# A tiled recurrence with a feed-forward layer: three leading blocks loaded, turned and ordered in another way

## The chip, the core and the metric

The kernel runs on one core of a Trainium2 chip. A core has a tensor engine (PE, which multiplies matrices and turns tiles), a vector engine (DVE), a scalar engine (ACT, for exponentials, logarithms and SiLU), a general engine (POOL) and SP, whose queue starts most transfers. Each engine works through its own list of instructions in order; semaphores hold an instruction back until what it needs is there. [...] The metric is the device time of one run in microseconds (us). Lower is better.

## What is computed

The first half is a gated recurrence over 768 tokens for 4 batches and 8 heads of 48 channels, the second a feed-forward layer on its output (3072 tokens of 384 channels, 2048 hidden).

```python
f = 1.0 / (1.0 + np.exp(-f_logit))
for t in range(S):
    state = f[:, :, t, :, None] * state + np.einsum('bhd,bhe->bhde', k[:, :, t], v[:, :, t])
    y[:, :, t] = np.einsum('bhd,bhde->bhe', q[:, :, t], state)
...
h = x @ w_in
g = h * (1.0 / (1.0 + np.exp(-h)))
return (g @ w_out).astype(np.float32)
```

Inputs and output are fp32.

## The kernel before

**Units.** A unit is 128 tokens of one batch with all its heads; there are 24, worked on in pairs. For each unit the recurrence is done with matrix products. `E` and `L` make the log of the gates on ACT (an exponential, then a logarithm); `cs` (or `csh`) sums them over the tokens on PE with a triangular matrix; `a`, `ia` and `al` are exponentials of the sums; `qg` and `ki` multiply q and k by them; `tq` turns both on PE into PSUM, and `qc`, `kc` or `qkc` copy the result to SBUF (units from 8 on use a transposing DMA, `qkD`, instead); `sc2` makes the scores of a pair, `at` masks them on the way out of PSUM, and `y` sums scores times v and the turned q times the state of the batch's last unit. `d`, `sd` and `su` bring that state on.

**Feed-forward.** `yc`, `yT` and `xc` (or `yD`, again a transposing DMA) turn y; `mi1` (units 0 to 5, one unit at a time, 12 matmuls of 128 columns, a quarter of the hidden layer) or `mi` (a pair, 6 matmuls of 256 columns, an eighth) make the hidden layer, `si1` and `si` apply SiLU on ACT, and `mo` adds a quarter of the output (4 matmuls of 384 columns). `oc` and `so` copy and store it. The weights come in fp32 through `wi` and `wo` into staging tiles and are cast by `wic` and `woc`.

**The first three pairs** (units 0 to 5) are loaded as blocks of 256 successive tokens of one batch: partition p of a tile gets tokens 2p and 2p+1, so that a piece of memory is 384 bytes. Each of the two slots of such a tile holds the tokens of one parity, of both units. v was loaded in the plain way, token by partition, and the turned k was put back into token order by a copy with a stride of two (`kc`), while q was left sorted by parity (`qc`).

**The order** of all engines is written out by hand, as a long table of words (`PLAN`): a word is the step, its unit, its engine and the buffers that it takes. The program emits the steps in that order, engine by engine; ACT gets a table load where exponentials and SiLU follow one another. Idle matmuls on zeros (`idle`) fill places in the head.

Steps in the code: loads L257, weights L295 and L299, `E` L264, `L` L266 (blocks) and L268, `idle` L291, `csh` L335 to L339, `cs` L372 and L376, `ia` L379, `a` L381, `tq` L395, the transposing DMAs L407 and L442, `dT` L411, `at` L416, `y` L422 and L426, `yT` L434, `d` L448, `sd` L453 and L455, `mi1` L313, `si1` L310, `mi` L323, `si` L320, `mo` L351, the last halves of `mo` L357, stores L364 and L369. Copies, casts and products stand at the lines of helpers: L235 (ACT), L237 (DVE), L239 (POOL), L242 (products).

Of the kernel before, what the change touches and what calls it, by code (L numbers as in the profile page):

```python
# [36 lines left out]
kn_0/ACT/0 d_0/PE/2 wi_1/SP/0 wi_0/SP/1 at_0_1/DVE/0 at_0_0/DVE sd_0/DVE/0 at_1_0/DVE/1 su_0/POOL/0 idle_4_2_256/PE/1 y_0/PE/3 tq_3/PE/1,5
idle_5_2_256/PE/2 tq_2/PE/2,0 wo_0/SP/1 a_4/ACT/1 ia_5/ACT/1 al_4/ACT/2 kc_3/ACT/1 at_1_1/DVE qc_3/DVE vb_1/ACT/1 a_5/ACT/2 yc_0/ACT/0 ia_4/ACT/2
kc_2/DVE qc_2/DVE y_1/PE/7 dT_2/PE/5 yT_0/PE/1 sc2_1/PE/6,0,3,2 wo_1/SP/2 wic_2_2/POOL wic_2_0/POOL yc_1/DVE/1 wic_2_1/ACT vb_2/ACT/2 xc_0/DVE/0
at_2_0/DVE/2 at_2_1/DVE dT_1/PE/4 yT_1/PE/7 dT_3/PE/1 mi1_0_1/PE/6 wi_4/SP/3 y_2/PE/0 xc_1/ACT wic_1_0/ACT wic_0_0/ACT kn_1/DVE/1 kn_2/DVE/0  # L40
yc_2/DVE/2 at_3_0/DVE/3 wic_1_1/POOL wic_0_1/POOL mi1_1_1/PE/7 d_2/PE/4 yT_2/PE/5 mi1_0_0/PE/0 mi1_1_0/PE/3 wi_3/SP/4 si1_0_1/ACT/0 si1_1_0/ACT
si1_0_0/ACT sd_2/DVE/1 xc_2/DVE/1 woc_0_2/DVE woc_0_1/DVE woc_0_0/DVE v_3/SP woc_1_2/DVE mi1_2_1/PE/4 mi1_2_0/PE/5 mo_1_0/PE/6 mo_0_0/PE/3 d_1/PE/0
si1_2_1/ACT/1 si1_2_0/ACT kn_3/ACT/0 woc_1_0/POOL si1_1_1/ACT wic_4_0/POOL wic_4_1/POOL wic_4_2/ACT at_3_1/DVE woc_1_1/DVE su_2/DVE/0 wic_3_1/DVE
sd_1/DVE/0 wic_3_2/POOL mo_2_0/PE/4 q_4_5/SP/2 k_4_5/SP/2 mo_1_1/PE mo_0_1/PE mo_2_1/PE mi1_0_3/PE/5 mi1_2_3/PE/1 mi1_1_3/PE/2 wo_2/SP/0 wic_3_0/ACT
vb_3/POOL/3 mi1_1_2/PE/7 y_3/PE/0 si1_0_3/ACT si1_2_3/ACT si1_1_2/ACT yc_3/DVE/0 qg_4/POOL/4 wo_3/SP/1 mi1_2_2/PE/5 d_3/PE/1 ki_4/POOL sd_3/DVE/1
yT_3/PE/7 mi1_0_2/PE/0 si1_2_2/ACT si1_0_2/ACT xc_3/DVE tq_4/PE/5,1 mi1_3_3/PE/7 mi1_3_2/PE/0 kc_4/ACT/2 si1_1_3/ACT qc_4/DVE si1_3_3/ACT si1_3_2/ACT
qg_5/DVE/0 ki_5/POOL tq_5/PE/5,1 mi1_3_0/PE/2 mi1_3_1/PE/7 f_6/SP/3 v_4/SP/2 f_8_9/SP/0 v_5/SP f_7/SP qc_5/ACT si1_3_0/ACT si1_3_1/ACT woc_2_2/POOL
woc_2_0/DVE woc_2_1/DVE kc_5/DVE mo_2_2/PE sc2_2/PE/0,5,2,1 dT_4/PE/7 mo_0_2/PE at_5_1/DVE/0 su_3/DVE/0 su_1/DVE/0 kn_4/DVE/1 at_5_0/DVE at_4_0/DVE/1
at_4_1/DVE woc_3_1/ACT woc_3_0/POOL woc_3_2/POOL vb_4/POOL/4 E_6/ACT L_6/ACT/0 E_8_9/ACT q_6/SP/3 v_6/SP/3 k_6/SP/3 mo_2_3/PE mo_1_2/PE mo_3_0/PE/1
mo_0_3/PE cs_6/PE/7 mo_3_1/PE d_4/PE/2 y_4/PE/0 a_6/ACT/0 L_8_9/ACT/1 yc_4/ACT/1 E_7/ACT ia_6/ACT/0 vb_5/DVE/5 oc_0/DVE/0 sd_4/DVE/1 su_4/DVE/0  # L50
mo_3_2/PE cs_9/PE/5 cs_8/PE/3 yT_4/PE/2 mo_1_3/PE y_5/PE/0 L_7/ACT al_9/ACT/3 al_6/ACT/4 a_8/ACT/1 ia_9/ACT/2 al_8/ACT/5 ia_8/ACT/1 a_9/ACT/2
oc_1/ACT/1 xc_4/DVE/2 yc_5/DVE/2 f_10_11/SP/1 q_7/SP k_7/SP q_8_9/SP/0 k_8_9/SP/0 f_12_13/SP/2 v_7/SP cs_7/PE/2 dT_5/PE/7 mo_3_3/PE yT_5/PE/0
kn_5/DVE/0 xc_5/DVE qg_6/POOL/1 ki_6/POOL vb_6/POOL/0 ia_7/ACT/0 a_7/ACT/0 al_7/ACT/6 E_10_11/ACT L_10_11/ACT/2 mi1_4_0/PE/3 mi1_4_1/PE/7 d_5/PE/5
tq_6/PE/6 qkc_6/DVE/0 oc_3/DVE/2 sd_5/DVE/0 oc_2/DVE/3 qg_7/DVE/3 ki_7/DVE mi1_4_2/PE/0 mi1_5_2/PE/2 mi1_5_1/PE/6 d_6/PE/1 mi1_4_3/PE/5 mi1_5_0/PE/4
si1_4_2/ACT/2 si1_5_1/ACT si1_4_0/ACT si1_5_0/ACT mi1_5_3/PE/0 tq_7/PE/6 mo_4_0/PE/3 mo_5_0/PE/4 sd_6/DVE/1 qkc_7/DVE qg_9/POOL/2 su_6/POOL/0
so_2/POOL v_8_9/SP/0 si1_5_3/ACT si1_4_1/ACT si1_5_2/ACT si1_4_3/ACT sc2_3/PE/1,0,6,7 q_12_13/SP/1 ki_8/POOL/4 at_6_1/DVE/2 ki_9/DVE at_6_0/DVE
at_7_1/DVE/3 at_7_0/DVE so_3/POOL vb_7/POOL/2 mo_5_1/PE cs_11/PE/2 mo_4_1/PE cs_10/PE/5 mo_4_2/PE y_6/PE/0 mo_4_3/PE d_7/PE/1 y_7/PE/7 E_12_13/ACT
al_11/ACT/7 a_10/ACT/0 L_12_13/ACT/1 al_10/ACT/0 yc_6/DVE/0 yc_7/ACT/1 oc_4/DVE/4 qg_8/POOL sd_7/DVE/1 cs_12/PE/6 cs_13/PE/0 yT_6/PE/3 mo_5_2/PE
yT_7/PE/1 ia_11/ACT/0 a_12/ACT/2 ia_12/ACT/1 ia_13/ACT/2 al_13/ACT/1 a_13/ACT/1 al_12/ACT/4 vb_9/POOL/1 xc_6/DVE/3 xc_7/DVE mo_5_3/PE mi_3_3/PE/7
d_9/PE/3 qkD_9/SP/1 qkD_8/SP f_14_15/SP/0 qg_12/DVE/0 su_7/POOL/0 vb_8/POOL/3 oc_5/DVE/3 sd_9/DVE/1 q_10_11/SP/2 k_10_11/SP/1 a_11/ACT/2 mi_3_0/PE/1  # L60
mi_3_4/PE/0 mi_3_5/PE/6 mi_3_6/PE/4 mi_3_1/PE/2 si_3_3/ACT/0 si_3_4/ACT si_3_5/ACT si_3_0/ACT si_3_1/ACT si_3_6/ACT su_5/POOL/0 qg_11/POOL/1
sc2_4/PE/3,7,0,6 mi_3_2/PE/1 mi_3_7/PE/2 at_9_0/DVE/1 at_8_1/DVE/0 at_8_0/DVE at_9_1/DVE si_3_2/ACT si_3_7/ACT mo_7_0/PE/4 mo_7_1/PE y_8/PE/0 y_9/PE/7
mo_7_2/PE mo_7_3/PE mo_6_0/PE/1 yc_8/DVE/2 ki_11/DVE qg_10/DVE/3 E_14_15/ACT yc_9/ACT/0 L_14_15/ACT/0 ia_10/ACT/0 ki_10/POOL k_12_13/SP/2 v_10_11/SP/1
qkD_11/SP/2 qkD_10/SP yT_9/PE/3 yT_8/PE/2 mo_6_1/PE cs_15/PE/6 mo_6_2/PE a_15/ACT/2 ia_15/ACT/0 al_15/ACT/6 xc_9/DVE/0 xc_8/DVE mi_4_1/PE/0
mi_4_0/PE/7 mi_4_2/PE/5 mi_4_3/PE/3 mi_4_6/PE/2 d_8/PE/6 mo_6_3/PE si_4_2/ACT/1 vb_10/ACT/4 si_4_1/ACT si_4_0/ACT si_4_3/ACT si_4_6/ACT sd_8/DVE/0
ki_12/DVE vb_11/DVE/5 v_14_15/SP/2 f_16_17/SP/3 k_14_15/SP/3 q_14_15/SP/3 mi_4_5/PE/5 mi_4_4/PE/0 sc2_5/PE/6,7,3,2 oc_6/DVE/2 qg_13/POOL/2 so_0/POOL
ki_13/POOL so_1/POOL su_9/POOL/0 qg_15/POOL/4 si_4_4/ACT si_4_5/ACT at_10_1/DVE/2 at_10_0/DVE at_11_0/DVE/3 su_8/POOL/0 at_11_1/DVE mo_8_0/PE/1
mi_4_7/PE/0 si_4_7/ACT cs_14/PE/5 mo_8_1/PE y_10/PE/7 mo_8_2/PE y_11/PE/6 d_11/PE/3 mo_9_0/PE/0 yc_10/DVE/1 yc_11/DVE/0 al_14/ACT/2 oc_7/ACT/0
E_16_17/ACT L_16_17/ACT/2 yT_10/PE/2 mo_8_3/PE yT_11/PE/7 mo_9_1/PE cs_16/PE/4 xc_10/ACT/1 oc_8/ACT/1 ia_14/ACT/2 a_16/ACT/0 al_16/ACT/3 a_14/ACT/1
ia_16/ACT/1 qg_14/POOL/1 xc_11/DVE sd_11/DVE/1 mi_5_3/PE/6 d_10/PE/2 mi_5_6/PE/7 mo_9_2/PE mi_5_4/PE/1 mi_5_1/PE/3 mi_5_0/PE/5 si_5_6/ACT/2 si_5_3/ACT  # L70
si_5_4/ACT si_5_0/ACT si_5_1/ACT qkD_13/SP/0 qkD_12/SP v_12_13/SP/3 q_16_17/SP/0 ki_14/DVE sd_10/DVE/0 su_10/DVE/0 ki_15/DVE qkD_15/SP/1 so_5/SP
qkD_14/SP f_18_19/SP/1 mi_5_2/PE/4 sc2_6/PE/2,7,6,1 mi_5_5/PE/5 mo_9_3/PE mi_5_7/PE/3 vb_13/POOL/0 at_12_1/DVE/0 at_13_1/DVE/1 vb_12/ACT/2 si_5_2/ACT
vb_14/DVE/1 su_11/POOL/0 at_13_0/DVE at_12_0/DVE si_5_7/ACT si_5_5/ACT d_12/PE/7 cs_17/PE/4 mo_11_0/PE/1 mo_11_1/PE mo_11_2/PE y_12/PE/6 d_13/PE/3
mo_10_0/PE/2 y_13/PE/5 mo_10_1/PE sd_12/DVE/0 yc_12/DVE/2 oc_9/DVE/3 sd_13/DVE/1 yc_13/DVE/1 a_17/ACT/2 al_17/ACT/5 ia_17/ACT/2 vb_15/ACT/3 yT_12/PE/7
mo_10_2/PE yT_13/PE/4 sc2_7/PE/6,0,3,5 E_18_19/ACT xc_12/DVE/2 su_13/DVE/0 L_18_19/ACT/1 xc_13/DVE f_20_21/SP/2 so_7/SP v_16_17/SP/0 v_18_19/SP/1
k_16_17/SP/0 at_14_1/DVE/2 at_15_0/DVE/3 at_15_1/DVE at_14_0/DVE mo_10_3/PE mi_6_1/PE/7 mi_6_7/PE/4 mi_6_6/PE/0 mo_11_3/PE y_14/PE/3 y_15/PE/5
# [454 lines left out]
```

## Time and profile before

| | |
|---|---|
| median of 3 runs | 178.46 us (177.73 to 179.22) |
| the profiled execution | 177.89 us |
| its span, first to last instruction | 176.1 us |
| read from memory, written | 25.17 MB, 4.72 MB |
| mean rate | 200 GB/s |
| DMA packets | 115541, of them 110752 under 512 bytes |
| ACT table loads | 18, 1.28 us each |

A profile's row in order of time has start, duration, engine, line, operation, output <- input, shapes and count, and in brackets how long the engine was idle before and what ended that. In rows of groups, the first number behind the bar is the busy time, the second the mean duration in ns of one. The chain of waits is followed back from the last instruction: at each step to what released it. Neighbouring matmuls overlap, so the pace of a row of matmuls is told by the time from start to start.

### The profile page before, as it was taken

What the parts mean: (1) busy time and instruction counts of PE and PEld (TensorE: products, weight loads), DVE (VectorE), ACT (ScalarE), POOL (GpSimd) and SP (SyncE); (2) the same over time, 40 slices, a digit from 0 to 9 for tenths busy, and PEclk for the clock granted to TensorE, in tenths of its full rate; (3) what the DMA queues carried; (4) which work ended last, traced back from release to release, by engine and by line L of the source; (5) the groups of instructions that cost most, each with busy time, mean ns of one, the idle gap of its engine ahead of it and who ended that gap; (6) DMA issues with size and microseconds to landing.
All of it is one profiled execution on the core that took longest, in us unless ns stands there. A gap on an engine that the chain in (4) does not pass through costs nothing.

```text
span 176.1 us, 4798 instructions
## 1 busy us (share of the span) xinstructions
PE 169.5 (96%) x1952; PEld 133.6 (76%) x1952; DVE 97.7 (55%) x201; ACT 133.3 (76%) x249; POOL 59.1 (34%) x91
## 2 busy tenths in 40 slices
PE   7998799999999999999999999999999999999992
...
PEclk9999999999999999999999999999999999999999
DMA  5999998998999999999899994999675975950222
GB/s 147 325 286 259 397 387 220 397 207 169 217 199 241 182 238 221 159 233 232 152 197 165 251 227 89 273 176 210 137 153 99 206 162 138 217 147 0 92 90 89
DMA packets 115541, 35.17 MB, mean 200 GB/s; under 512 B 110752, under 2 KB 113056, under 8 KB 115520
## 3 DMA queue, kind: packets, MB, share of 16 engines
...
q8 instruction: 15, 0.25, 0.5%
...
HBM read 25.17 MB, written 4.72 MB: 170 GB/s over the span
## 4 chain that ended last, share of the span: by engine, by line
PE 73%; SPq 8%; DMA 8%; DVE 5%; issue 2%; POOL 2%; ACT 0%; POOLq 0%; DVEq 0%
PE ps L351 27%; PE ps L323 22%; PE ps L313 8%; SPq L257 6%; DMA wh<-in_moe_w_in_dram 5%; PE ps L280 3%; PE ps L357 3%; DMA qkT<-qk 3%; PE ps L426 2%; SPq L442 2%; DVE st L242 2%; PE ps L422 2%; PE ps L372 1%; DVE at L416 1%; PE ps L448 1%
## 5 line engine op out<-in xcount | busy, mean ns | idle before, releaser
L351 PE MATMUL ps<-w_out,hT 128*128 128x384 bf16 x352 | 66.4, 326 | 0.0
L323 PE MATMUL ps<-xT,w_in 128*128 128x256 bf16 x432 | 52.4, 273 | 0.0
L323 PEld LDWEIGHTS <-w_in 128*128 128x128 bf16 x432 | 45.3, 110 | 3.9 <-DMA xT<-yb 0.3
L320 ACT ACTIVATE hT<-ps 128x512 bf16<-128x512 f32 x72 | 39.0, 603 | 10.3 <-PE ps L323 9.6
L351 PEld LDWEIGHTS <-hT 128*128 128x128 bf16 x352 | 31.7, 97 | 16.6 <-ACT hT L310 0.3
L416 DVE TENSOR_TENSOR at<-ps,triu 128x512 bf16<-128x512 f32 x36 | 22.5, 683 | 19.8 <-PE ps L280 18.8
L242 POOL TENSOR_TENSOR qk<-q,av 128x384 bf16<-128x384 f32 x15 | 15.4, 1033 | 42.2 <-DMA q<-in_q_dram 25.0
L499 ACT ACT_TABLE_LOAD x17 | 21.8, 1283 | 0.3
L313 PE MATMUL ps<-xT,w_in 128*128 128x128 bf16 x288 | 17.9, 219 | 0.9 <-POOL w_in L239 0.6
L313 PEld LDWEIGHTS <-w_in 128*128 128x128 bf16 x288 | 16.6, 110 | 1.3 <-POOL w_in L239 0.8
L242 POOL TENSOR_TENSOR qk<-k,ia 128x384 bf16<-128x384 f32 x12 | 12.7, 1066 | 13.4 <-DMA k<-in_k_dram 8.7
L381 ACT ACTIVATE av<-ps 128x384 f32<-128x384 f32 x24 | 11.9, 504 | 3.5 <-PE ps L376 1.8
L237 DVE CAST yb<-ps 128x384 bf16<-128x384 f32 x16 | 8.8, 555 | 10.2 <-PE ps L426 9.0
L264 ACT ACTIVATE f<-f 128x768 f32<-128x768 f32 (+1 forms) x13 | 10.3, 796 | 5.4 <-DMA f<-in_f_logit_dram 5.3
L310 ACT ACTIVATE hT<-ps 128x512 bf16<-128x512 f32 x24 | 13.2, 607 | 1.6 <-PE ps L313 1.5
L453 DVE TENSOR_TENSOR sd<-ps,st 128x384 f32<-128x384 f32 x16 | 8.8, 553 | 9.5 <-ACT hT L320 4.7
L369 POOL DMA_DIRECT2D out_dram<-ob x14 | 8.0, 573 | 17.9 <-DVE ob L237 14.3
L242 POOL TENSOR_TENSOR st<-sd,al 48x192 bf16<-48x192 f32 x18 | 9.8, 543 | 8.7 <-PE ps L422 5.1
L379 ACT ACTIVATE ia<-ps 128x384 f32<-128x384 f32 x24 | 11.8, 505 | 0.0
L237 DVE COPY ob<-ps 128x384 f32<-128x384 f32 x14 | 7.7, 553 | 7.4 <-PE ps L351 3.6
L239 POOL CAST vb<-v 128x384 bf16<-128x384 f32 x11 | 5.6, 507 | 14.6 <-DMA v<-in_v_dram 13.2
L242 DVE TENSOR_TENSOR qk<-k,ia 128x384 bf16<-128x384 f32 x12 | 7.1, 605 | 5.1 <-ACT ia L379 4.2
...
## 6 DMA issues: line engine op xcount, KB each, us to landing
...
```

The costliest lines, as they stand in the source:

```text
L237: nc.vector.tensor_copy(o, i)
L242: (nc.vector if eng == "DVE" else nc.gpsimd).tensor_mul(*a)
L257: nc.sync.dma_start(out=dst, in_=src)
L310: return nc.scalar.activation(at("hT", u // 2)[:, 4 * m:4 * m + 4, i * C:(i + 1) * C], h, AF.Silu)
L313: nc.tensor.matmul(h[:, n, :], w_in_tile(4 * m + n, kk), at("xT", u // 2)[:, kk, i * C:(i + 1) * C], start=(kk == 0), stop=(kk == KT - 1))
L320: return nc.scalar.activation(at("hT", P)[:, 2 * j:2 * j + 2, :], h, AF.Silu)
L323: nc.tensor.matmul(h[:, i, :], w_in_tile(2 * j + i, kk), at("xT", P)[:, kk, :], start=(kk == 0), stop=(kk == KT - 1))
L351: nc.tensor.matmul(o, at("hT", P)[:, n, i * C:(i + 1) * C], w_out_sb[n // 4][:, n % 4, :], start=(n == 0), stop=(n == NT - 1))
L379: nc.scalar.activation(at("ia", u).rearrange("p h d -> p (h d)"), at("cs", u)[:, 0:HD], AF.Exp)
L381: nc.scalar.activation(at("av", u).rearrange("p h d -> p (h d)"), at("cs", u)[:, 0:HD], AF.Exp, scale=-1.0)
L416: nc.vector.tensor_mul(at("at", u)[:, r], at(f"s{r}", u).rearrange("p (n c) -> p n c", c=C), (triup if two else triu)[:, None, :].to_broad ...
L499: nc.scalar.preload_act_table_set(turn[n])
```

## The change

- `v` of units 0 to 5 is loaded sorted by parity, in two DMAs of 64 partitions each; the turned q and k then both stay sorted, and one copy (`qkc`) takes both out of one PSUM bank. The mask `triup` is built to match.
- `E` and `L` of the three blocks work on half of the heads at a time (`Eh`, `Lh`), and a load may take half of the heads: `f_0_1` is loaded so, heads 4 to 7 first.
- The set `BLOCKS` replaces the number `HALF` (the same three pairs), and `APART` goes. Weights may be loaded straight by POOL, and scores one unit at a time; the new table uses neither.
- `PLAN` is new throughout: engines, buffers and order.

```diff
-HALF = 3
-
-APART = {0, 1, 2, 3, 4, 5}
+BLOCKS = {0, 1, 2}
...
-f_0_1/SP/0 f_2_3/SP/1 k_0_1/SP/0 q_0_1/SP/0 E_0_1/ACT L_0_1/ACT/0 E_2_3/ACT idle_0_11_512/PE/0 csh_0/PE/0,1 f_4_5/SP/2 q_2_3/SP/1 v_0/SP/0 k_2_3/SP/1
...
+f_0_1_1/SP/0 f_0_1_0/SP f_2_3/SP/1 q_2_3/SP/0 q_0_1/SP/1 k_0_1/SP/0 Eh_0_0/ACT Eh_0_1/ACT Lh_0_1/ACT/0 Lh_0_0/ACT idle_0_12_512/PE/0 csh_0/PE/0,1
...
-        if u // 2 < HALF and n == 2:
...
+        if u // 2 in BLOCKS and n >= 2:
+            hs = slice(0, H) if n == 2 else slice(4 * us[2], 4 * us[2] + 4)
+            dst = at(x, u // 2).rearrange("p a h d -> p (a h d)").rearrange("p (h w) -> p h w", h=H)[:, hs]
+            src = SRC[x][b, hs, c * C:(c + 2) * C, :].rearrange("h (p s) d -> p h (s d)", s=2)
+        elif u // 2 in BLOCKS:
+            for s in range(2):
+                nc.sync.dma_start(out=at(x, u // 2)[64 * s:64 * (s + 1), u % 2],
+                                  in_=SRC[x][b, :, c * C:(c + 1) * C, :].rearrange("h (p s) d -> s p h d", s=2)[s])
+            return
...
+    def half_logs(kind, u, hf):
+        P, hs = u // 2, slice(4 * hf, 4 * hf + 4)
+        if kind == "Eh":
+            e = at("f", P).rearrange("p a h d -> p (a h d)").rearrange("p (h w) -> p h w", h=H)[:, hs]
+            nc.scalar.activation(e, e, AF.Exp, scale=-1.0)
+        else:
+            nc.scalar.activation(at("lf", P)[:, :, hs, 0:D], pairs("f", P)[:, :, hs], AF.Ln, bias=1.0)
...
         elif kind == "qkc":
-            copy(eng, at("qkT", P)[:, 1024 * i:1024 * (i + 1)], bank16("tq", u))
-        elif kind in ("qc", "kc"):
...
-            copy(eng, dst, bank16("tqk" if j and u in APART else "tq", u)[:, 512 * j:512 * (j + 1)].rearrange("p (w c) -> p w c", c=64))
+            if two:
+                copy(eng, at("qkT", P).rearrange("p (w s c) -> p s w c", s=2, c=64)[:, i],
+                     bank16("tq", u).rearrange("p (w c) -> p w c", c=64))
+            else:
+                copy(eng, at("qkT", P)[:, 1024 * i:1024 * (i + 1)], bank16("tq", u))
...
-        nc.vector.tensor_copy(triup.rearrange("p (s c) -> p s c", s=2), triu.rearrange("p (c s) -> p s c", s=2))
...
+        for s in range(2):
+            r = slice(64 * s, 64 * (s + 1))
+            nc.vector.tensor_copy(triup[r, 64:128], tri2[r, r])
+            nc.vector.tensor_copy(triup[r, 0:64], (tri2s if s else tri2)[r, r])
```

What the table moves is seen best in the lists of the engines. On SP's queue, from the last loads of the first two pairs on to the weights, the program of before has (tiles f_71, q_78 and k_74 are those of pair 2 or 1; ws and wh stage weights):

```order
L257 DMA f_71<-in_f_logit_dram 128x8x96
L257 DMA q_78<-in_q_dram 128x8x96
L257 DMA v_81<-in_v_dram 128x8x48
L257 DMA k_74<-in_k_dram 128x8x96
L257 DMA v_82<-in_v_dram 128x8x48
L257 DMA v_81<-in_v_dram 128x8x48
L295 DMA ws_85<-in_moe_w_in_dram 128x3x512
L295 DMA wh_90<-in_moe_w_in_dram 128x3x256
```

And the changed one:

```order
L262 DMA k_73<-in_k_dram 128x8x96
L262 DMA k_74<-in_k_dram 128x8x96
L256 DMA v_81<-in_v_dram 64x8x48 x2
L262 DMA f_71<-in_f_logit_dram 128x8x96
L256 DMA v_81<-in_v_dram 64x8x48 x2
L256 DMA v_82<-in_v_dram 64x8x48 x2
L316 DMA ws_85<-in_moe_w_in_dram 128x3x512
L316 DMA ws_86<-in_moe_w_in_dram 128x3x512
```

The third block's f moves behind the k of the first two, each v comes as two halves, and two large weight loads follow one another where a large one and two small ones did.

On ACT, at the start (f_69 is the gate tile of pair 0, f_70 of pair 1), before:

```order
L264 ACTIVATE f_69<-f_69 128x768
L266 ACTIVATE lf_92<-f_69 128x16x48
L264 ACTIVATE f_70<-f_70 128x768
L266 ACTIVATE lf_93<-f_70 128x16x48
L379 ACTIVATE ia_95<-ps_61 128x384
```

And now:

```order
L279 ACTIVATE f_69<-f_69 128x384 x2
L281 ACTIVATE lf_92<-f_69 128x2x4x48 x2
L279 ACTIVATE f_70<-f_70 128x384 x2
L281 ACTIVATE lf_93<-f_70 128x2x4x48 x2
L404 ACTIVATE av_98<-ps_61 128x384
```

Each step has become two, and `a` comes ahead of `ia`.

On DVE, between the first states and the first output weights (sd_122 and sd_123 are sums for a state, w_in_160 to 162 and w_out_163 the cast weights, yb and xT the y of units), before:

```order
L237 CAST yb_121<-ps_61 128x384
L416 TENSOR_TENSOR at_118<-ps_64,triup 128x512
L455 COPY sd_123<-ps_65 128x384
L237 COPY xT_140<-ps_66 128x3x2x64
L237 CAST w_out_163<-ws_86 128x512 x3
L237 CAST w_out_164<-ws_87 128x512
```

And now:

```order
L236 CAST w_in_162<-ws_86 128x512 x2
L241 TENSOR_TENSOR st_147<-sd_123,al_124 48x4x48 x2
L435 TENSOR_TENSOR at_118<-ps_63,triup 128x512
L236 CAST w_in_160<-ws_87 128x512 x2
L236 CAST w_in_159<-wh_90 128x384
L236 CAST w_in_158<-wh_91 128x384
L236 CAST w_out_163<-ws_88 128x512 x3
L236 CAST vb_109<-v_82 128x384
L236 CAST w_out_164<-ws_89 128x512
```

All of the hidden layer's weights are cast before the output's, DVE casts six pieces of them where it cast one, and the v of unit 3 (vb_109) is cast between the first and the second output weight.

More of the change, by code (lines that the diff above doesn't have):

```diff
@@ L37 @@
[L37 to L76, printed above, removed]
@@ L101 @@
-moh_23_0_0/PE/2 moh_23_0_1/PE moh_23_0_2/PE moh_23_0_3/PE moh_22_0_2/PE moh_22_0_3/PE moh_22_1_1/PE moh_22_1_2/PE moh_22_1_3/PE moh_23_1_1/PE
-och_22_0/ACT/3 och_23_0/ACT/1 oc_18/DVE/4 och_22_1/ACT moh_23_1_2/PE moh_23_1_3/PE so_18/SP so_21/POOL so_20/POOL soh_23_0/SP soh_22_1/SP soh_22_0/SP
-och_23_1/ACT soh_23_1/SP
+f_0_1_1/SP/0 f_0_1_0/SP f_2_3/SP/1 q_2_3/SP/0 q_0_1/SP/1 k_0_1/SP/0 Eh_0_0/ACT Eh_0_1/ACT Lh_0_1/ACT/0 Lh_0_0/ACT idle_0_12_512/PE/0 csh_0/PE/0,1
+Eh_2_1/ACT Eh_2_0/ACT Lh_2_1/ACT/1 Lh_2_0/ACT k_2_3/SP/1 v_0/SP/0 f_4_5/SP/2 v_1/SP v_2/SP/1 idle_1_5_256/PE/2 csh_1/PE/2,3 a_0/ACT/0 a_1/ACT/1
@@ new lines @@
+at_1_0/DVE kn_1/DVE/0 wi_2/SP/2 at_2_0/DVE/2 at_2_1/DVE dT_3/PE/1 d_1/PE/6 yT_0/PE/7 d_2/PE/4 y_1/PE/0 xc_0/ACT/0 Lh_4_0/ACT kn_3/DVE/0 wi_1/SP/0
+wi_0/SP/1 wic_3_2/POOL wic_3_0/POOL y_2/PE/3 yc_1/ACT/1 yc_2/DVE/2 wic_3_1/ACT csh_2/PE/7,1 yT_2/PE/0 yT_1/PE/3 xc_2/ACT/1 sd_2/DVE/1 at_3_1/DVE/3
+sd_1/DVE/0 xc_1/ACT mi1_0_2/PE/4 mi1_2_2/PE/5 mi1_1_2/PE/0 wic_4_0/ACT wo_0/SP/3 wic_4_2/DVE wic_4_1/DVE su_2/DVE/0 at_3_0/DVE wo_1/SP/4 mi1_1_3/PE/3
+mi1_2_3/PE/6 mi1_0_3/PE/2 wic_2_2/POOL si1_1_2/ACT/0 si1_0_2/ACT wic_2_1/DVE wic_2_0/DVE si1_1_3/ACT si1_0_3/ACT si1_2_3/ACT/1 wic_1_1/DVE
```

128 lines of the change are left out of this document (85 added, 43 removed).

## The prediction

> **What bounds the kernel now.** I read the page first: busy time of the engines and the 40 slices.
>
> ```profile
> span 176.1 us, 4798 instructions
> ...
> PE 169.5 (96%) x1952; PEld 133.6 (76%) x1952; DVE 97.7 (55%) x201; ACT 133.3 (76%) x249; POOL 59.1 (34%) x91
> ...
> PE   7998799999999999999999999999999999999992
> ...
> PEclk9999999999999999999999999999999999999999
> DMA  5999998998999999999899994999675975950222
> ```
>
> The tensor engine (PE) is busy everywhere but in the first five slices (22 us) and the last; its clock is full in all of them. The change takes no matrix work away: the order of both programs has the same matmuls, save the idle ones on zeros (26 before, 31 now). So its end moves only by time in which it does nothing useful. I read the chain of waits next, for where that time ends.
>
> ```profile
> 12.72 8.02 DMA wh<-in_moe_w_in_dram
> ...
> 20.77 0.52 ACT w_in L235
> ...
> 21.34 2.85 PE ps L313 x48
> ...
> 25.66 2.65 PE ps L351 x16
> 28.31 2.68 PE ps L313 x48
> ...
> 173.02 0.32 ACT ob L235
> ```
>
> Up to 21.34 the chain runs through the queue of SP and a weight transfer; from there nearly all of it is PE work, to 173.0. The rows also price a step: 2.65 / 4 = 0.66 us for one `mo` (4 matmuls) and 2.68 / 4 = 0.67 us for one `mi1` (12 matmuls). PE's timeline shows the head.
>
> ```profile
> 5.98 0.32 PE L335 MATMUL ps<-lf,tri 128*128 128x384 bf16 x1 [0.22 <-ACT lf L266]
> ...
> 11.89 0.62 PE L280 MATMUL ps<-qkT 48*128 48x128 bf16 x16
> ...
> 17.03 0.62 PE L280 MATMUL ps<-qkT 48*128 48x128 bf16 x16
> ...
> 18.96 0.86 PE L313 MATMUL ps<-xT,w_in 128*128 128x128 bf16 x12 [0.59 <-POOL w_in L239]
> 19.66 0.36 PE L426 MATMUL ps<-vb,at 128*128 128x48 bf16 x8
> ...
> 20.54 0.33 PE L448 MATMUL ps<-vb,kn 128*128 128x96 bf16 x4
> 20.71 0.33 PE L434 MATMUL ps<-ident,yb 128*128 128x128 bf16 x3
> ```
>
> First scores at 11.89, second at 17.03, first hidden layer (`mi1`) at 18.96, waiting for weights. What sets that is when the weights land: the instructions that cast each piece stand idle until its DMA.
>
> ```profile
> 17.64 0.62 ACT L235 CAST w_in<-ws 128x512 bf16<-128x512 f32 x1 [0.78 <-DMA ws<-in_moe_w_in_dram]
> ...
> 22.73 1.10 DVE L237 CAST w_out<-ws 128x512 bf16<-128x512 f32 x3 [0.55 <-DMA ws<-in_moe_w_out_dram]
> ...
> 24.67 0.87 POOL L239 CAST w_out<-ws 128x512 bf16<-128x512 f32 x1 [3.36 <-DMA ws<-in_moe_w_out_dram]
> 26.70 1.18 POOL L239 CAST w_in<-ws 128x512 bf16<-128x512 f32 x2 [1.15 <-DMA ws<-in_moe_w_in_dram]
> 29.25 0.87 POOL L239 CAST w_in<-ws 128x512 bf16<-128x512 f32 x1 [1.38 <-DMA ws<-in_moe_w_in_dram]
> ```
>
> Six weight loads of 768 KB (the two 384 KB ones count as one, at 20.77 in the chain) land at 17.6, 20.8, 22.7, 24.7, 26.7 and 29.2 us. Each gives PE three units' work, 3 x 0.67 = 2.0 us, so loads and work run at almost the same pace.
>
> **The change, part by part.**
>
> *Does the first weight land earlier?* It is behind the same pieces on SP. Its queue:
>
> ```profile
> 7.79 1.15 SPq L257 DMA_DIRECT2D k<-in_k_dram  x1
> 8.99 2.03 SPq L257 DMA_DIRECT2D v<-in_v_dram  x2
> 11.06 1.08 SPq L295 DMA_DIRECT2D ws<-in_moe_w_in_dram  x1
> 12.18 1.03 SPq L295 DMA_DIRECT2D wh<-in_moe_w_in_dram  x2
> ```
>
> A `k` of 384 KB holds it 1.15 us, a `v` of 192 KB 2.03 / 2 = 1.02, a `wh` of 384 KB 0.52. The first two have 1024 pieces each (128 partitions x 8 heads), `wh` 384. Cost follows pieces, not bytes. Halving a load (`f_0_1`, and three `v` ahead of the weights) keeps the pieces, so I take nothing; from above, halves at the `wh` price of 0.52 would add 3 x (2 x 0.52 - 1.02) = 0.06 us, and the worst case is a rival below. Below nothing, no piece goes away. The first weight still lands at 17.6.
>
> *Exponentials and logarithms by halves.* One whole pair on ACT:
>
> ```profile
> 4.21 0.84 ACT L264 ACTIVATE f<-f 128x768 f32<-128x768 f32 x1 [2.19 <-DMA f<-in_f_logit_dram]
> 5.08 0.84 ACT L266 ACTIVATE lf<-f 128x768 bf16<-128x768 f32 x1
> 5.83 0.83 ACT L264 ACTIVATE f<-f 128x768 f32<-128x768 f32 x1
> ...
> 7.44 0.85 ACT L379 ACTIVATE ia<-ps 128x384 f32<-128x384 f32 x2
> ```
>
> Two of 384 columns take 0.85 us, one of 768 takes 0.84: halving costs 0.01 us each time. The gain would be an earlier start, but the second half of the heads is loaded first while ACT starts with the first half, so it still waits for both, until 4.2. The chain of four then ends near 6.0 as before (5.92): term 0, between -0.4 (half a load less to wait for) and +0.2. [...]
>
> *Turned q and k in one copy.*
>
> ```profile
> L237 DVE COPY qkT<-ps 128x512 bf16<-128x512 bf16 x8 | 4.2, 570 | 0.3 <-PE ps L395 0.2
> ...
> L237 DVE COPY qkT<-ps 128x1024 bf16<-128x1024 bf16 x2 | 1.4, 692 | 1.8 <-PE ps L395 1.8
> ```
>
> Two copies of 0.57 become one of 0.69: 0.45 us less for each unit that DVE copies, and one PSUM bank less. Larger is what the order does with it. The k of units 2 and 3 came late:
>
> ```profile
> 12.76 1.95 POOL L242 TENSOR_TENSOR qk<-k,ia 128x384 bf16<-128x384 f32 x2
> ```
>
> It was done at 14.7, and the second scores came 2.3 us behind. Now `k_2_3` is loaded two places sooner (2 x 1.15 us) and DVE makes both; then the last of the four is unit 3's q on POOL (1.0 us), near 13.0, and 2.3 us more put the second scores at about 15.3. So `d_1`, `d_2`, `y_2` and `yT_2` are done when the first weight is there. By the starts above a `d` or `yT` is 0.17 us (20.54 to 20.71) and a `y` without a state 20.54 - 0.67 - 19.66 = 0.21, so 0.72 for the four. Before, `d_1` came later still, and the other three (0.55) lay with two `mi1` (1.34) between 18.96 and 21.34: 2.38 - 1.34 - 0.55 = 0.49 us of waiting for the next weights. With three `mi1` at hand on the first load, that wait isn't met at once. So the head can win 0.72 + 0.49 = 1.2 us: the same 18.96 with more behind it, and no hole right after.
>
> *What is late next.* The new order lets all 12 `mi1` of units 0 to 2 run ahead of the `mo`, on the six landings. PE would be through the first load's work at 18.96 + 2.01 = 20.97. The second is there at 20.8 and its two casts on DVE take some 0.8 (three took 1.10): PE starts at 21.6, waiting 0.65. Third: 22.7 + 0.85, PE free at 23.6: no wait. Fourth, 24.7 + 0.9: 25.6 against 25.6. Fifth: 26.7 + 1.1 = 27.8 against 27.6, 0.2. Then three `mo` to 29.8, and `y_3` needs `v_3`, which lands last:
>
> ```profile
> 16.28 2.33 SPq L257 DMA_DIRECT2D v<-in_v_dram  x1
> ...
> DMA to landing us min/median/max: 13.5/13.5/13.5
> ```
>
> 16.28 + 13.5 = 29.8; its cast, 0.4: PE waits some 0.4 us, since `y_3` stands ahead of two `mo` that could run (the old order put it behind them). Sum of what is given back: 0.65 + 0.2 + 0.4 = 1.25; bounds 0.4 (the second load lands 0.8 sooner, as nothing small is in it) to 2.0.
>
> *The old order's own holes.* After 28 us PE has a few of its own.
>
> ```profile
> 32.89 0.91 PE L395 MATMUL ps<-ident,qk 128*128 128x128 bf16 x8
> ...
> 34.97 0.61 PE L395 MATMUL ps<-ident,qk 128*128 128x128 bf16 x8
> ```
>
> The turning of unit 4 takes 0.30 us more than that of unit 5: its k is late from POOL. In the new order DVE makes that k, with time to spare. I take 0.3 won, between 0 and 0.6, since the steps around it move too.
>
> *The middle and the end.* One hole is a transposing DMA:
>
> ```profile
> PEld L280 <- DMA qkT<-qk: 0.3, 1, 0.3
> ...
> L407 SPq DMA_TRANSPOSE qkT<-qk x16: 1231/1269/3565, 57.0 to 148.7; - x16
> ```
>
> Everything else is moved, with two ACT table loads more (1.28 each), under which PE has other work. The last scores come closer behind their transposes: by the plan's listing some 3.9 us of PE work lies between the two, 7.8 before. I take 0 for the middle, between -0.3 and +2.5. The end (half `mo`, copy, store) is the same.
>
> **Sum** against the profiled execution, 177.89 us (span 176.1 and 1.8 around it): -1.2 + 1.25 - 0.3 = -0.25, so 177.6. That is 0.5% under the median of the runs shown, 178.46. They spread from 177.7 to 179.2, so about 1% is what a measurement of this kernel can tell from no change.
>
> **Rivals.**
>
> *The weights keep up* (faster): none of the 1.25 us comes back. For it: the second landing of before was two loads of 384 KB, and a single one may be quicker. 177.89 - 1.2 - 0.3 = 176.4, 1.2% under the median.
>
> *Halves of v cost as much as whole ones* (slower): each of the three extra `v` DMAs ahead of the weights holds the queue 1.15 us. For it: 64 partitions and 192-byte pieces are a form the trace does not show, and `k` and `v` cost about the same at twice the bytes. Against it: `wh`, at 0.52. The weights land 3 x 1.15 = 3.5 us late, PE waits all of it: 177.6 + 3.5 = 181.1. It counts from 0.9 us more for each `v` (3 x 0.9 = 2.6 above the forecast). [...]
>
> *Transposes late in the middle* (slower): pair 5's scores now follow pair 4's after 6 us of PE work instead of 13, and the last are close, too. If three of these places wait 1 us each, 177.6 + 3 = 180.6; it needs 0.9 us at each to count. Against it: one load instead of five now stands on SP between pair 4's transposes and pair 5's.
>
> *The head does nothing* (the halves are late anyway, the two copies were hidden, weights rule): 177.9, no change.
>
> **How the numbers follow.** Forecast 177.6: 0.34. Head does nothing, 177.9: 0.20. Weights keep up, 176.4: 0.24. Transposes late, 180.6: 0.12. Halves of v, 181.1: 0.10. Faster by over 1% (under 176.7): 0.24. Slower by over 1% (over 180.2): 0.22. Within: 0.54. The range takes in the gains at their bounds (177.89 - 1.2 - 0.6 - 0.3 in the middle = 175.8) and reaches up to the first of the slower rivals, where about half of their chance lies: 175.8 to 180.6.
>
> **What would show it.** Right, if the first `mi1` starts within 0.5 us of 18.96 with four more steps behind it, the second scores start near 15.3, and PE has holes before the second load's `mi1` and before `y_3`. The halves of `v` are told by when SP comes to the first weight load, 11.06 before. Wrong, if that passes 12, if the first scores pass 12.4, or if PE shows waits of over 0.7 us ahead of scores after 50 us. If the first `mi1` of unit 4 starts over 1 us sooner than before, the give-back was overrated.

## The result, and the profile after

| | before | after |
|---|---|---|
| median of 20 runs each | 178.16 us (177.16 to 179.22) | 179.53 us (178.46 to 181.48) |
| ratio, 95% interval | 1 | 1.0074 (1.0048 to 1.0100) |
| the profiled execution, its span | 177.89, 176.1 us | 178.59, 176.8 us |

The changed kernel is 0.7% slower, some 1.3 us. The forecast was 177.6, a small gain. The page of the changed kernel shows PE as full as before:

```profile
span 176.8 us, 4813 instructions
...
PE 170.2 (96%) x1957; PEld 134.4 (76%) x1957; DVE 103.3 (58%) x210; ACT 138.2 (78%) x257; POOL 47.4 (27%) x74
```

SP's queue in order of time (start, time that the issue held the queue) shows where the difference begins. Before, up to the first v:

```profile
0.74 1.08 SPq L257 DMA_DIRECT2D f<-in_f_logit_dram  x2
1.87 1.11 SPq L257 DMA_DIRECT2D k<-in_k_dram  x1
3.02 1.15 SPq L257 DMA_DIRECT2D q<-in_q_dram  x1
4.21 1.15 SPq L257 DMA_DIRECT2D f<-in_f_logit_dram  x1
5.41 1.15 SPq L257 DMA_DIRECT2D q<-in_q_dram  x1
6.60 1.15 SPq L257 DMA_DIRECT2D v<-in_v_dram  x1
```

And now, up to the weights:

```profile
0.74 1.55 SPq L262 DMA_DIRECT2D f<-in_f_logit_dram  x3
2.33 3.05 SPq L262 DMA_DIRECT2D q<-in_q_dram  x2
5.43 2.34 SPq L262 DMA_DIRECT2D k<-in_k_dram  x2
7.81 1.85 SPq L256 DMA_DIRECT2D v<-in_v_dram  x2
9.71 0.62 SPq L262 DMA_DIRECT2D f<-in_f_logit_dram  x1
10.38 3.12 SPq L256 DMA_DIRECT2D v<-in_v_dram  x4
13.54 1.68 SPq L316 DMA_DIRECT2D ws<-in_moe_w_in_dram  x3
```

The same bytes go out, but SP comes to the first weight at 13.54 instead of 11.06, 2.48 us late. Half of that is there at the first v (7.81 instead of 6.60): the two q hold SP for 3.05, where two loads of that size took 2.30 before. The other half comes from there to the first weight (5.73 us instead of 4.46), with the three v in halves. Here the hold of one load isn't its price: the halves hold 4.97 where whole ones took 1.15 + 2.03, but the f between them holds only 0.62 where the k of before took 1.15. So places several loads further on are compared below. PE's own timeline, and the chain of waits up to the end of the head:

```profile
13.40 0.62 PE L293 MATMUL ps<-qkT 48*128 48x128 bf16 x16 [0.70 <-DVE qkT L236]
...
17.18 0.62 PE L293 MATMUL ps<-qkT 48*128 48x128 bf16 x16
...
21.01 8.20 PE L334 MATMUL ps<-xT,w_in 128*128 128x128 bf16 x144
...
32.21 0.36 PE L445 MATMUL ps<-vb,at 128*128 128x48 bf16 x8 [0.44 <-DVE vb L236]
```

```profile
2.96 2.43 SPq L262
...
20.15 0.61 SPq L256
...
20.80 10.90 DMA v<-in_v_dram
...
31.80 0.37 DVE vb L236
...
32.21 0.36 PE ps L445 x8
32.56 0.77 PE ps L374 x4
```

Followed back from the end, the chain is PE work to 32.21, then unit 3's v, its transfer of 10.90 us, and from there SP's issues one after the other to the start; the longest is the second q, 2.43. Before, it left the loads at 21.34, with a weight. So in the new order the last load that the head needs, not a weight, releases PE. Ahead of its first `mi1` at 21.01 PE shows no wait; it comes there late from the scores, which start at 13.40 instead of 11.89.

### The profile page after: what moved, and what is told of

It reads as the page before. It is cut to its first block, busy times and chain, and to the rows that moved or that the text cites. A ratio compares the mean times of both kernels' runs of the same rounds, so it can differ in the third digit from the quotient of the medians.

```text
span 176.8 us, 4813 instructions
## 1 busy us (share of the span) xinstructions
PE 170.2 (96%) x1957; PEld 134.4 (76%) x1957; DVE 103.3 (58%) x210; ACT 138.2 (78%) x257; POOL 47.4 (27%) x74
## 3 DMA queue, kind: packets, MB, share of 16 engines
q0 software_dynamic: 576, 1.77, 2.9%
## 4 chain that ended last, share of the span: by engine, by line
PE 80%; SPq 11%; DMA 6%; issue 1%; DVE 0%; ACT 0%; DVEq 0%
PE ps L374 32%; PE ps L344 27%; DMA v<-in_v_dram 6%; PE ps L334 5%; SPq L262 4%; PE ps L293 3%; SPq L256 3%; PE ps L380 3%; PE ps L445 2%; SPq L316 2%; PE ps L441 2%; PE ps L395 2%; PE ps L467 2%; SPq L320 1%; PE ps L453 1%; PE ps L418 1%
## 5 line engine op out<-in xcount | busy, mean ns | idle before, releaser
L374 PE MATMUL ps<-w_out,hT 128*128 128x384 bf16 x352 | 65.0, 326 | 0.0
L341 ACT ACTIVATE hT<-ps 128x512 bf16<-128x512 f32 x72 | 38.5, 603 | 11.5 <-PE ps L344 11.2
L241 POOL TENSOR_TENSOR qk<-q,av 128x384 bf16<-128x384 f32 x12 | 13.2, 1110 | 36.8 <-ACT av L404 25.1
L236 DVE COPY ob<-ps 128x384 f32<-128x384 f32 (+1 forms) x15 | 7.7, 527 | 14.2 <-PE ps L374 8.3
L241 DVE TENSOR_TENSOR st<-sd,al 48x192 bf16<-48x192 f32 x24 | 13.9, 577 | 0.8 <-PE ps L441 0.6
L241 POOL TENSOR_TENSOR st<-sd,al 48x192 bf16<-48x192 f32 x16 | 8.9, 554 | 18.9 <-DVE sd L472 11.6
L331 ACT ACTIVATE hT<-ps 128x512 bf16<-128x512 f32 x24 | 12.8, 602 | 0.9 <-PE ps L334 0.7
L241 DVE TENSOR_TENSOR qk<-q,av 128x384 bf16<-128x384 f32 x12 | 9.1, 762 | 6.6 <-ACT av L404 6.5
L241 POOL TENSOR_TENSOR qk<-k,ia 128x384 bf16<-128x384 f32 x8 | 8.3, 1043 | 15.2 <-DMA k<-in_k_dram 10.4
L236 DVE CAST yb<-ps 128x384 bf16<-128x384 f32 x13 | 6.9, 552 | 7.7 <-PE ps L445 5.9
L241 DVE TENSOR_TENSOR qk<-k,ia 128x384 bf16<-128x384 f32 x16 | 9.5, 610 | 2.8 <-DMA k<-in_k_dram 2.1
```

The lines of the kernel that those rows point to most:

```text
L236: nc.vector.tensor_copy(o, i)
L241: (nc.vector if eng == "DVE" else nc.gpsimd).tensor_mul(*a)
L331: return nc.scalar.activation(at("hT", u // 2)[:, 4 * m:4 * m + 4, i * C:(i + 1) * C], h, AF.Silu)
L341: return nc.scalar.activation(at("hT", P)[:, 2 * j:2 * j + 2, :], h, AF.Silu)
L374: nc.tensor.matmul(o, at("hT", P)[:, n, i * C:(i + 1) * C], w_out_sb[n // 4][:, n % 4, :], start=(n == 0), stop=(n == NT - 1))
```

## The experiments

The ratios are to the kernel before, with 95% intervals. "SP" is the time at which SP comes to the first weight load, "`mi1`" the start of the first hidden layer, from one profiled execution each. That execution can lie away from the median (by 1.6 us for f in halves: 178.22 against 179.80), so the sizes are read from the ratios and the places from the profile. In the three runs of the changed order with v in one piece and the copy as it was (third, fifth and fourteenth row) v no longer matches the sorted scores, so their output is not the right one; the work is the same.

| run | ratio | SP | `mi1` |
|---|---|---|---|
| before | 1 | 11.06 | 18.96 |
| after | 1.0074 (1.0048 to 1.0100) | 13.54 | 21.01 |
| after, v in one piece | 0.9973 (0.9938 to 1.0008) | 11.99 | 21.27 |
| after, f in one piece | 1.0000 (0.9963 to 1.0037) | 12.22 | 20.12 |
| after, both in one piece | 0.9950 (0.9918 to 0.9982) | 11.36 | 20.08 |
| after, `E` and `L` whole | 1.0071 (1.0037 to 1.0106) | 13.93 | 21.74 |
| before, v in halves of partitions | 1.0061 (1.0025 to 1.0097) | 12.85 | 20.38 |
| before, v in halves of heads | 1.0027 (0.9992 to 1.0062) | 11.86 | 19.34 |
| before, f in halves of heads | 1.0066 (1.0032 to 1.0100) | 11.59 | 19.54 |
| before, second q in halves of heads | 1.0023 (0.9990 to 1.0056) | 11.05 | 18.59 |
| after, copy before k | 1.0065 (1.0031 to 1.0099) | 13.27 | 21.60 |
| after, f in one piece, copy before k | 0.9996 (0.9961 to 1.0030) | 12.26 | 19.21 |
| the same, third unit's v earlier | 1.0004 (0.9970 to 1.0038) | 12.23 | 19.05 |
| after, both in one piece, copy before k | 0.9965 (0.9934 to 0.9997) | 11.00 | 19.30 |
| after, order of the tokens | 1.0083 (1.0047 to 1.0120) | 11.05 | 21.03 |
| the same without its waits for copies | 1.0000 (0.9981 to 1.0020) | 10.94 | 20.19 |
| the same, second pair sorted | 1.0062 (1.0028 to 1.0095) | 11.76 | 19.72 |

### Undoing the splits

v in one transfer:

```diff
-            for s in range(2):
-                nc.sync.dma_start(out=at(x, u // 2)[64 * s:64 * (s + 1), u % 2],
-                                  in_=SRC[x][b, :, c * C:(c + 1) * C, :].rearrange("h (p s) d -> s p h d", s=2)[s])
-            return
+            dst = at(x, u // 2)[:, u % 2]
+            src = SRC[x][b, :, c * C:(c + 1) * C, :].rearrange("h s d -> s h d")
```

> The changed kernel, but each v of the first three pairs comes in one transfer over 128 partitions, tokens in their own order (so v's rows no longer match the sorted scores, and the output differs). Theory 1, the halves of v are what makes the weights late: SP comes to the first weight load at about 11.9 us instead of 13.5 (three v at 1.02 instead of about 1.6), the first hidden layer starts about 1.5 us sooner than 21.0, and the time falls by 0.6 to 1.0 us, to about 178.7. Theory 2, the two halves of f at the start slow the loads behind them: SP still passes 13 us at the first weight load, and the time stays near 179.5. Theory 3, the exponentials by halves: no change.

f in one transfer:

```diff
-f_0_1_1/SP/0 f_0_1_0/SP f_2_3/SP/1
+f_0_1/SP/0 f_2_3/SP/1
```

> The changed kernel, but the f of the first pair comes in one transfer. Theory 1 (halves of v): the first weight load stays near 13.5 us and the time near 179.5. Theory 2 (halves of f slow the loads behind them): the next three loads go at 1.15 us each, the second f is there by 5.8 instead of 6.6, SP comes to the first weight load near 12.5, and the time falls by 0.4 to 0.8 us. Theory 3: no change.

Whole exponentials and logarithms:

```diff
-Eh_0_0/ACT Eh_0_1/ACT Lh_0_1/ACT/0 Lh_0_0/ACT
+E_0_1/ACT L_0_1/ACT/0
...
-Eh_2_1/ACT Eh_2_0/ACT Lh_2_1/ACT/1 Lh_2_0/ACT
+E_2_3/ACT L_2_3/ACT/1
```

> The changed kernel, but exponentials and logarithms of the first two pairs are done for all heads at once. Theory 3 (halves cost 0.1 us each on ACT): the first a starts about 0.2 us sooner, the first scores too, and the time falls by 0.1 to 0.3 us. Theories 1 and 2: the first weights set the first hidden layer, so its start and the time stay within 0.2 us of 21.0 and 179.5.

Theories 1 and 2 both hold, by more time than they said: undoing v gives back 1.0%, undoing f 0.7%. Undoing the halves on ACT gives back nothing that can be told; the 0.1 to 0.3 us of theory 3 are less than the interval of 0.6 us to each side. The start of the first hidden layer was a bad mark: with v whole it comes later (21.27) and the program is still faster, as PE no longer waits for the last v. Then both splits were undone:

> The changed kernel with f of the first pair in one transfer and each v of the first three pairs in one over 128 partitions (v's tokens in their own order, so the output differs). If the two splits cost independently, the gains of the two single runs add (0.74% and 1.0%): ratio to the kernel before about 0.990, SP at the first weight load near 11 us, no wait before the third unit's y. If both had delayed the same thing, the ratio stays near that of the better one, 0.997.

The gains overlap: 1.0074 to 0.9950 is 1.2%, not 1.7%. With both loads whole the rest of the change (order, one copy, halves on ACT) is 0.5% faster than before. This gain is small: the medians of all runs, 177.86 against 178.32 us, make it 0.3%. The scores of the third pair and the last ones, in the changed kernel and then in this run, show that the two runs differ by the head alone:

```profile
41.53 0.62 PE L293 MATMUL ps<-qkT 48*128 48x128 bf16 x16
...
155.05 0.62 PE L293 MATMUL ps<-qkT 48*128 48x128 bf16 x16
```

```profile
39.59 0.62 PE L291 MATMUL ps<-qkT 48*128 48x128 bf16 x16
...
153.10 0.62 PE L291 MATMUL ps<-qkT 48*128 48x128 bf16 x16
```

1.94 us apart at 41 us, 1.95 at 155.

### Adding the splits to the kernel before

The loads of v, in halves of partitions, and the same with `dst[:, 4 * s:4 * (s + 1)]` for halves of heads:

```diff
+            if u // 2 < HALF:
+                for s in range(2):
+                    nc.sync.dma_start(out=dst[64 * s:64 * (s + 1)], in_=src[64 * s:64 * (s + 1)])
+                return
```

> The kernel before, but each v of the first three pairs comes in two transfers of 64 partitions (tokens in their own order). Theory 1: the three v ahead of the weights hold SP some 1.6 us each instead of 1.02, SP comes to the first weight load near 12.8 instead of 11.06, the first hidden layer starts 1 us or more after 18.96, and the time rises by 0.5 to 1.5 us over 178.2. Theory 2: SP stays within 0.3 us of 11.06 and the time within 0.3 us of the kernel before.

> The kernel before, but each v of the first three pairs comes in two transfers of 128 partitions and four heads. If the 64 partitions are what costs, SP comes to the first weight load within 0.3 us of 11.06 and the time is that of the kernel before. If any second transfer costs, the weights are as late as with halves of 64 partitions (12.85 us), and the ratio is near 1.006.

SP's queue with halves of partitions, and with halves of heads:

```profile
6.85 1.84 SPq L259 DMA_DIRECT2D v<-in_v_dram  x2
8.73 0.74 SPq L261 DMA_DIRECT2D k<-in_k_dram  x1
9.52 3.29 SPq L259 DMA_DIRECT2D v<-in_v_dram  x4
12.85 0.62 SPq L299 DMA_DIRECT2D ws<-in_moe_w_in_dram  x1
13.52 1.61 SPq L299 DMA_DIRECT2D wh<-in_moe_w_in_dram  x2
```

```profile
6.57 1.76 SPq L259 DMA_DIRECT2D v<-in_v_dram  x2
8.37 0.51 SPq L261 DMA_DIRECT2D k<-in_k_dram  x1
8.92 2.89 SPq L259 DMA_DIRECT2D v<-in_v_dram  x4
11.86 0.51 SPq L299 DMA_DIRECT2D ws<-in_moe_w_in_dram  x1
12.41 1.02 SPq L299 DMA_DIRECT2D wh<-in_moe_w_in_dram  x2
```

With halves of 64 partitions SP is 1.79 us late at the first weight load; 0.25 of that was there ahead of the first v, so the three v take 1.54 more (0.51 for each). With halves of heads it is 0.80 late there, but the weight load behind holds it 0.51 instead of 1.08, and at the next one (12.18 before) it is 0.23 late, against 1.34 with halves of partitions. When the first weight lands says the same. Its first cast, 17.64 before, starts in the two runs at:

```profile
19.06 0.62 ACT L235 CAST w_in<-ws 128x512 bf16<-128x512 f32 x1 [1.00 <-DMA ws<-in_moe_w_in_dram]
```

```profile
18.02 0.62 ACT L235 CAST w_in<-ws 128x512 bf16<-128x512 f32 x1 [1.19 <-DMA ws<-in_moe_w_in_dram]
```

So the halves of partitions cost, and whether a second transfer costs by itself isn't shown. In time, the 0.6% for halves of partitions is clear of no change; the 0.3% for halves of heads is not. The halves of the changed kernel also pick every second token from memory, which no run takes apart; on SP they are no dearer (5.68 us from the first v to the first weight in the run with f in one piece, 6.00 here).

> The kernel before, but the f of the first pair comes in two transfers of four heads, heads 4 to 7 first; the exponential still takes it whole. If the split slows the loads behind it whatever the order of the program, the next loads of 1024 pieces hold SP 1.4 us or more instead of 1.15, SP comes to the first weight load at 12 us or later instead of 11.06, and the ratio is 1.003 to 1.008. If the slow loads came from the changed order of the loads, SP stays within 0.3 us of 11.06 and the ratio is 1.000.

> The kernel before, but the q of the second pair, the fifth load, comes in two transfers of four heads. If any split of a load slows the loads behind it, SP comes to the first weight load at 11.5 us or later instead of 11.06, and the ratio is 1.003 to 1.007, as with f in two. If the slow loads come from a split at the very start of the queue, SP stays within 0.2 us of 11.06 and the ratio at 1.000.

The edit is the same loop over heads 4 to 7 and 0 to 3, for that one load. SP's queue with f in halves:

```profile
0.74 1.00 SPq L256 DMA_DIRECT2D f<-in_f_logit_dram  x2
1.79 0.50 SPq L261 DMA_DIRECT2D f<-in_f_logit_dram  x1
2.33 0.58 SPq L261 DMA_DIRECT2D k<-in_k_dram  x1
2.96 1.74 SPq L261 DMA_DIRECT2D q<-in_q_dram  x1
4.74 1.15 SPq L261 DMA_DIRECT2D f<-in_f_logit_dram  x1
```

The loss is in one place, the fifth transfer: 1.74 us, where a load of that size takes 1.15. In the four runs of the changed order with f in halves the same place has 1.77 to 2.43. From then on SP is 0.53 us late. A q in halves further back makes SP no later (11.05). So it is not any split; a split at the start of the queue costs. Two limits: in three of the twelve runs behind the 1.0066 the granted clock was 0.990, and the other nine alone give about 1.0045; and in the profiled execution the third pair's scores come at 37.39, no later than 37.51 before, so where PE loses the time isn't shown.

The rate at which the core's DMA moves data shows both splits. From 4 to 8 us it is 322 to 325 GB/s in nine runs with f of the first pair whole (325 in the kernel before) and 260, 293 and 295 in three with it in halves. The pages of the other five show the same in their second slice (4.4 to 8.8 us): 324 to 325 with f whole, 279 and 294 with it in halves. From 8 to 16 us it is 237 to 255 in three runs where the three v come in halves of partitions, and 264 to 295 in the nine where they come whole or in halves of heads (271 before, 276 with halves of heads). So the issues aren't merely late: less data moves meanwhile. Whether the slower issues cause that or follow from it, and why the fifth transfer is the one held, isn't settled.

### What bounds the head of the new order

In the changed kernel DVE does unit 3's k, which waits for its load, ahead of unit 1's copy, on which the first scores wait. The two were exchanged:

```diff
-tq_1/PE/5 ki_3/DVE/2
-qkc_0/ACT/0 qkc_1/DVE
+tq_1/PE/5
+qkc_0/ACT/0 qkc_1/DVE ki_3/DVE/2
```

> The changed kernel with two steps exchanged on DVE: the copy of unit 1's turned q and k comes ahead of unit 3's k, which waits for its load (0.67 us at 12.05). If that wait is what holds the first scores back (the copy behind it ended at 13.26, the scores started at 13.40), they start at 12.5 to 12.8, and if the head hangs on them the time falls by 0.3 to 0.7 us (ratio 1.003 to 1.006 to the kernel before). If the weights hold the head, the first hidden layer stays at 21.0 and the ratio at 1.007.

> The changed kernel with f of the first pair in one transfer and the same two steps exchanged on DVE. With f whole the ratio was 1.000, and the copy ended at 12.15 behind a k that waited until 11.0. If the first scores hold the head, they start near 11.3 instead of 12.29, the first hidden layer 0.5 to 1 us sooner than 20.12, and the ratio is 0.994 to 0.997. If the weights (landed near 18.1, cast until 19.9) hold it, the first hidden layer stays within 0.2 us of 20.1 and the ratio near 1.000.

With f in halves the scores start at 13.28 instead of 13.40 and the ratio stays. This execution doesn't tell why: the two products ahead of the copy took DVE 1.83 us, where they took 1.03 in the changed kernel. With f whole the first scores come at 11.46 and the first hidden layer at 19.21, 0.9 us sooner than in the run with f whole alone, and the time doesn't move. PE's timeline shows where that went:

```profile
27.89 2.46 PE L374 MATMUL ps<-w_out,hT 128*128 128x384 bf16 x12 [0.17 <-DVE w_out L236]
...
31.58 0.36 PE L445 MATMUL ps<-vb,at 128*128 128x48 bf16 x8 [1.05 <-DVE vb L236]
```

With f whole alone the row at 31.58 stood at 31.30, with a wait of 0.72. It waits for the same load. Moving that v ahead of the second output weight, `v_3/SP wo_1/SP/4`:

> As the run before, and unit 3's v is loaded ahead of the second output weight instead of behind it, with unit 3's state product ahead of the output step that needs that weight. With f whole PE waited 0.72 us for this v, ahead of the second output weight. If the wait goes without a new one, 0.4 to 0.7 us less than the run before; if the weight is then as late as the v was, PE waits for it instead and the time stays within 0.2 us of the run before.

Here PE waits 0.94 us for the first output weight and 0.45 for the second instead: the wait has moved to the neighbouring loads. With v whole as well there is no such wait:

> The changed kernel with f and v whole (v's tokens in their own order, so the output differs) and the copy of unit 1 ahead of unit 3's k. With v in halves the exchange gained nothing (0.9996 against 1.000), though the first hidden layer came 0.9 us sooner: the last v was then waited for. If the loads set the end of the head, the exchange pays once v is quick: PE shows no wait ahead of the third unit's y, and the ratio falls from 0.995 to 0.988 to 0.992. If something else holds the head, it stays at 0.995.

The first hidden layer comes at 19.30 and no wait ahead of the third unit's y is left, as expected, but the ratio is 0.9965 against 0.9950, no gain that these intervals show. So the bound by the loads is shown for v in halves; why an earlier start wins nothing once they are whole is open.

### Keeping the order of the tokens instead

Halves of v are there because k is sorted by parity. The copy can put both back into token order, with v in one transfer and the output that of the reference:

```diff
-                copy(eng, at("qkT", P).rearrange("p (w s c) -> p s w c", s=2, c=64)[:, i],
+                copy(eng, at("qkT", P).rearrange("p (w c s) -> p s w c", s=2, c=64)[:, i],
```

> The changed kernel with f of the first pair in one transfer and v in one transfer of 128 partitions, where the one copy of the turned q and k puts both back into the order of the tokens (a stride of two), so that nothing stays sorted and the output is right. The loads go as in the run with both in one piece. If the strided copy costs what the plain one does (1.0 us on ACT, 0.68 on DVE), the ratio is near 0.990; if DVE takes 1.0 to 1.1 us for it, the second scores come 0.4 us later and the ratio is 0.991 to 0.997; in either case faster than the kernel before.

That was not met. The copies on ACT and DVE were dearer, and PE waited for them:

```profile
10.18 1.31 ACT L233 COPY qkT<-ps 128x1024 bf16<-128x1024 bf16 x1
...
11.54 1.28 DVE L235 COPY qkT<-ps 128x1024 bf16<-128x1024 bf16 x1
```

```profile
12.96 0.62 PE L290 MATMUL ps<-qkT 48*128 48x128 bf16 x16 [1.49 <-DVE qkT L235]
...
40.17 0.62 PE L427 MATMUL ps<-ident,qkT 128*128 128x128 bf16 x8 [0.91 <-DVE qkT L235]
```

Then the same with the copy before the k, and the third pair's turning moved behind other work:

> As the run in the order of the tokens (f and v whole, output right, strided copies of 1.28 us on DVE and 1.31 on ACT), with its two waits for copies taken out: unit 1's copy ahead of unit 3's k on DVE, the second cast of the third output weight ahead of the copies of units 4 and 5, and the turning of those units behind output steps that can run before. There PE waited 1.49 and 0.91 us for copies. If the copies were what made that run slow, the first scores start near 11.8 us instead of 12.96, pair 2's scores near 40 instead of 42.02, and the ratio is 0.988 to 0.997, faster than both kernels; if the loads set the head there too, they start no sooner and the ratio stays above 1.003.

1.0000 (0.9981 to 1.0020): 0.7% faster than the changed kernel, no faster than the one before. The scores came near their marks (12.12, and 40.23 for the third pair), but the ratio expected from them (0.988 to 0.997) wasn't reached. Going back to halves of v for the second pair alone:

> As the run in the order of the tokens without its waits for copies (ratio 1.000), but the second pair stays sorted by parity, with v of units 2 and 3 in halves: of the three v ahead of the weights one is halved, and the copies of units 2 and 3 take 1.0 and 0.68 us instead of 1.31 and 1.28. If the copies hold the second scores (0.65 us of waiting) and one halved v costs the loads some 0.66 us that PE does not wait for, the ratio is 0.996 to 0.999; if the loads hold the head, PE waits for the last v again and it stays at 1.000 or above.

This loses 0.6% again, with a wait of 0.52 us for unit 3's v: the case in which the loads hold the head. No run with the right output beat both kernels.

## Why the prediction was wrong, step by step

- **"Halving a load keeps the pieces, so I take nothing"** is the step that failed. It was priced at 0 to 0.06 us, from rows of whole loads, and "cost follows pieces" doesn't hold even there: the first two f, of 1024 pieces each, held SP 0.54 us each (1.08 for both), later loads of the same form 1.15. In the changed kernel SP is 2.48 us late and the first weight's first cast starts at 19.46 instead of 17.64; undoing both splits takes 2.18 of the 2.48 away and 1.2% (about 2.2 us) of the time. What is left of the change is 0.5%, about 0.9 us, faster than before; the difference is the 1.3 us measured.
- **"Faster by 0.5%"** was mostly no gain of the change: the sum gives 0.25 us, and 0.57 is the distance from the profiled execution (177.89) to the median of three (178.46).
- **The rival "halves of v cost as much as whole ones"** had the right sign, and its mark, SP past 12 us, was met, as was that of first scores past 12.4 (13.40). Its size, 1.15 us for each v, was too large: 0.51 in the kernel before, at a ratio of 1.0061. There the first v's two halves held SP for 1.84, a whole one 1.15. That f in halves would cost was in no rival.
- **Exponentials by halves at 0.01 us** was too small, though it changed nothing in the time that the runs can tell. ACT's rows of the changed kernel, two halves each time, and two `a` of the same width:

```profile
4.01 0.94 ACT L279 ACTIVATE f<-f 128x384 f32<-128x384 f32 x2 [1.99 <-DMA f<-in_f_logit_dram]
...
6.62 0.94 ACT L279 ACTIVATE f<-f 128x384 f32<-128x384 f32 x2 [0.71 <-DMA f<-in_f_logit_dram]
...
8.29 0.85 ACT L404 ACTIVATE av<-ps 128x384 f32<-128x384 f32 x2
```

  A pair of halves takes 0.94, 0.10 more than a whole (0.84). The row that priced it in the prediction, 0.85 for two, reads PSUM (the banks that the matmuls write, `ps` in the rows); the exponentials of f read SBUF, where a DMA put f. That the memory makes the difference is an inference from these rows; no run takes it apart. The wait of 0.71 at 6.62 is the slow load again.
- **Second scores at 15.3** came at 17.18. With f in one piece they come at 16.07, and with unit 1's copy ahead of unit 3's k as well at 15.24. So the slow loads took 1.1 us and a step that the prediction left out, the k on DVE that waits for its load ahead of the copy, 0.8. Of the copies, priced at DVE's 0.69, ACT makes one of each two, at 1.01; in that last run PE waits 0.36 us for it.
- **The head's gain of 1.2 us at an unchanged 18.96** didn't come: the first `mi1` starts at 21.01, at 20.08 with both loads whole, and at 19.30 with the copy ahead of the k too. Each time it comes 7.6 to 7.9 us behind the first scores (13.40, 12.47, 11.44), so here these set it, and not the first weight, as the prediction had it. **Of the give-back**, the wait for `y_3` came as said, behind the load that lands last; that its size agrees (0.44 against 0.4) is luck, since the load and PE were both some 2 us later than reckoned. The 0.65 and 0.2 ahead of the second and fifth weights weren't there, as `mi1` began later and ran through.
- **The hole at unit 4's turning** went, as said: the 16 matmuls of both units now run as one row of 1.06 us at 37.49. **The middle at 0** was about right, and the rival of late transposes fell: from 40 to 160 us PE is busy for all 120.0 us in the changed kernel (119.8 before), and after 50 us it shows no wait ahead of scores.
